# Trainium2, attention and FFN in one kernel: the written-out start is closed to later work, weights are converted in wider chunks, and the start's order is planned anew

## The chip, the cores and the metric

The kernel runs on one core of one Trainium2 chip. The metric is the device time of one execution in microseconds (us), the median of three. A core has five engines that run in parallel, each strictly in its own order: TensorE (PE in the profile) for matmuls, VectorE (DVE), ScalarE (ACT), GpSimd (POOL) and SyncE (SP), which here only issues DMA transfers. An instruction that needs another engine's result waits, and everything behind it on its engine waits with it.

## What is computed

```
x  = out_up + out_local                  # attention, 8 batches x 8 heads, 576 positions, 64 wide
     out_local: softmax over |i - j| < 4 (banded), times v
     out_up:    attention on means of 4 positions, each row repeated 4 times
x  -> (4608, 512)                        # rows = batch x position, columns = head x 64
h  = x @ w_in                            # (4608, 2048)
g  = s * relu(h)**2 + b
out = g @ w_out                          # (4608, 512)
```

`w_in` and `w_out` arrive as 64-bit floats, everything else in 32 bits.

## The kernel before

**FFN.** The 4608 rows are cut into 18 token tiles `t` of 256 and the 2048 FFN columns into 8 "f pairs" `p` of 256. One step `(t, p)` has four parts, which the written-out order calls by one letter. `G` is half of the first product: 12 matmuls into the accumulator `ph` (L622), so 24 for a step; values are split into a high and a low part and three products are summed. `R` is `upper`: Relu, Square and the high part `gh` on ScalarE (L635 to L637). `V` is `lower`: the low part `gl` on VectorE (L642), called the eviction below. `H` is half of the second product into `po` (L684 to L686), 6 matmuls. The term `b` is added at the end as `b` times the column sums of `w_out`: `add_rows(p)` adds up the rows of one pair's `wo` on VectorE (L656, L658, tile `bias`), four adds for a pair, and `column_sums` makes `cs` of them with one matmul (L662), ahead of the second product of step (0, 7).

**Weights.** The 64-bit values of pairs 0 to 6 land in staging tiles `wst` (1024 values a partition for `w_in` and as many for `w_out`) and are converted by `convert` in chunks of 512 columns, so two chunks of each. A chunk runs through ScalarE and VectorE in turn over a scratch tile `es`: scale (L246, ScalarE), two tensor-scalar operations (L248, L249, VectorE), two scalar-tensor-tensor operations (L251, L252, VectorE), a cast to the high part (L254, ScalarE), and the low part by subtraction (L258, VectorE). `es` is one of two buffers of the tag `pv`. Pair 7 is loaded in eight quarters of 256 columns into the same two `pv` buffers and converted by `split_w(7)`.

**Attention.** A unit is a pair of heads of one batch; its parts are `d` (the attention on means), `v` (the sums of `v`, on GpSimd) and `l` (the banded part). The result is `x`; `begin_x` splits the first two token tiles into `xh` and `xl` (L742, L744), `third_x` the third (L752, L754), into buffers of the tags `os` and `xl2`.

**What sets the order.** The order of the first 14 steps, of eight attention units and of pairs 0 to 6 is written out in the string `PLAN`: each word advances one stream (`c` and a number is a weight chunk, `d`, `l`, `v` and a number a unit, `x` and `y` are `begin_x` and `third_x`, then `G`, `R`, `V`, `H`). The instructions traced for it are chained by `in_order`, which makes each follow the one before it on its engine. What is traced afterwards (steps 14 onwards, `split_w(7)`, `add_rows`, the later units) is not chained: a list scheduler places it by priority, and may put it between instructions of the written-out order where it reckons that the engine would wait. The tail of that code:

```
    begin = 2 * HF
    for st in range(begin, len(order)):
        t, p = order[st]
        until("G", 2 * st + 2)
        ...
        if st == begin:
            split_w(NFP - 1)
        if st - begin < NFP:
            add_rows(st - begin)
```

The steps run in this order: tiles 0 and 1 over pairs 0 to 6 (the 14 of the written-out order), then tile 2 over pairs 0 to 6, then tiles 0 to 2 on pair 7, then one tile after the other.

Of the kernel before, what the change touches and what calls it, by code (L numbers as in the profile page):

```python
# [11 lines left out]
F32 = mybir.dt.float32  # L12
# [4 lines left out]
ALU = mybir.AluOpType  # L17
AX = mybir.AxisListType

P = 128  # L20
B, H, S, D = 8, 8, 576, 64
# [17 lines left out]
NFP = DFF // 256  # L39
# [8 lines left out]
NQ = SD // GQ  # L48

STAGE = (7, 6, 7, 6, 7, 6, 7)  # L50
CHUNK = 512
HF = 7
GROUPS = [(i // HP, i % HP // 2) for i in range(EU, B * HP, 2)]

W_MAX = (1.875 - 2.0 ** -23) * 2.0 ** (31 - 127)

PLAN = (
# [16 lines left out]
)  # L74

OB = {0: (0, 1), 1: (2, 3), 2: (6, 7)}
# [3 lines left out]
def attention_ffn_kernel(ctx, tc, qk, vw_in, vr_in, vdm, qkn, vn, w_in, w_out, s_in, b_in, out):  # L80
    nc = tc.nc
# [3 lines left out]
    one = ctx.enter_context(tc.tile_pool(name="one", bufs=1))  # L85
    two = ctx.enter_context(tc.tile_pool(name="two", bufs=2))
# [141 lines left out]
    def load_quarter(p, op, i):  # L228
        if op == "i":
            src = src_i[:, i, 512 * p : 512 * p + 512]  # L230
        else:
            src = src_o[:, 2 * p + i // 2, 512 * (i % 2) : 512 * (i % 2) + 512]
        st = two.tile([P, 256, 2], I32, tag="pv", name="wst")
        nc.sync.dma_start(st.rearrange("p f t -> p (f t)"), src)
        return st

    def convert(st, hi, lo, op, p):


        n = hi.shape[1]  # L240
        top, low = st[:, :, 1], st[:, :, 0]
        f = two.tile([P, n], F32, tag="pv", name="es")
        w = f.bitcast(I32)


        nc.scalar.mul(f, top.bitcast(F32), 2.0 ** -112)  # L246
        yield
        nc.vector.tensor_scalar(f, f, W_MAX, -W_MAX, ALU.min, ALU.max)  # L248
        nc.vector.tensor_scalar(w, w, 3, 0x7FFFFFF8, ALU.logical_shift_left, ALU.bitwise_and)  # L249
        yield  # L250
        nc.vector.scalar_tensor_tensor(w, low, 29, w, ALU.logical_shift_right, ALU.bitwise_or)  # L251
        nc.vector.scalar_tensor_tensor(w, top, -0x80000000, w, ALU.bitwise_and, ALU.bitwise_or)  # L252
        yield
        nc.scalar.copy(hi, f)  # L254
        yield
        for i in range(0, n, 512):
            js = slice(i, min(i + 512, n))
            nc.vector.tensor_tensor(lo[:, js], f[:, js], hi.bitcast(F32)[:, js], ALU.subtract)  # L258

    def split_w(p):  # L260
        for chunk in split_parts(p):
            for _ in chunk:
                pass

    def split_parts(p):
        wi[p] = one.tile([P, 2, NK, 256], F32R, tag=f"wi{p}", name="wi")
        wo[p] = one.tile([P, 2, 2, DM], F32R, tag=f"wo{p}", name="wo")
        for op, w in (("i", wi[p]), ("o", wo[p])):
            fl = w.rearrange("p s k f -> p s (k f)")
            if p < len(STAGE):  # L270
                st = wst.pop((p, op))
                for j in range(0, 1024, CHUNK):
                    js = slice(j, j + CHUNK)
                    yield convert(st[:, js], fl[:, 0, js], fl[:, 1, js], op, p)
            else:
                for i in range(4):
                    cs = slice(256 * i, 256 * i + 256)
                    yield convert(load_quarter(p, op, i), fl[:, 0, cs], fl[:, 1, cs], op, p)
# [311 lines left out]
    def split_x(t):  # L590
        tags = ("os", "xl2") if t == 2 else ("xh", "xl")
        pool = one if t == 2 else two
        xh = pool.tile([P, HP, TB], F32R, tag=tags[0], name="xh")
        xl = pool.tile([P, HP, TB], F32R, tag=tags[1], name="xl")
        t0 = t * TB
        while t0 < (t + 1) * TB:
            b = t0 // S
            while (b, HP - 1) not in complete:
                next(gen)
            n = min((t + 1) * TB, (b + 1) * S) - t0  # L600
            src = xt[b][:, :, t0 - b * S : t0 - b * S + n]
            dst = slice(t0 - t * TB, t0 - t * TB + n)
            nc.scalar.copy(xh[:, :, dst], src)
            nc.vector.tensor_tensor(
                xl[:, :, dst], src, xh[:, :, dst].bitcast(F32), ALU.subtract)
            t0 += n
        xs[t] = (xh, xl)
# [43 lines left out]
    def add_rows(p):  # L651


        parts = [wo[p][:, i // 2, i % 2].bitcast(F32) for i in range(4)]
        if p == 0:
            nc.vector.tensor_tensor(bias, parts.pop(), parts.pop(), ALU.add)  # L656
        for part in parts:
            nc.vector.tensor_tensor(bias, bias, part, ALU.add)  # L658
# [55 lines left out]
    tail = {}  # L714
    ENGINES = [e.engine for e in (nc.tensor, nc.vector, nc.scalar, nc.gpsimd)]
# [67 lines left out]
    def all_chunks():  # L783
        for p in range(HF):
            if p > 1:
                load_w(p)
            if 1 < p < 4:
                load_pair(1, p)
            yield from split_parts(p)
# [13 lines left out]
    with tc.high_priority(offset=400):  # L803
        with in_order():
            for name in plan:
                next(streams[name], None)

    gone = {kind: plan.count(kind) for kind in "GRVH"}

    def until(kind, count):  # L810
        while gone[kind] < count:
            next(streams[kind])
            gone[kind] += 1
# [19 lines left out]
    def target(st):  # L833
        return sum(
            min(1.0, max(0.0, (st - free[b]) / (need[b] - free[b]))) * NY[b]
            for b in range(1, B))

    def advance(st):
        nonlocal done
        while done < target(st):  # L840
            with tc.high_priority(offset=300 if done < NY[1] else 60 if done < NY[1] + NY[2] else 0):
                if next(gen, "end") == "end":
                    break
            done += 1

    splits = {(2, NFP - 2): 3}
    splits.update({(t, NFP - 3): t + 1 for t in range(3, NB - 1)})
    begin = 2 * HF
    for st in range(begin, len(order)):
        t, p = order[st]  # L850
        until("G", 2 * st + 2)
        with tc.high_priority():
            until("R", st + 1)
            until("V", st + 1)
        if st == begin:
            split_w(NFP - 1)
        if st - begin < NFP:
            add_rows(st - begin)
        advance(st + 0.5)
        until("H", 2 * (st + 1 - (2 if t < 3 else 3)))  # L860
        advance(st + 1)
        if (t, p) in splits:
            split_x(splits[t, p])
    until("H", 2 * len(order))


# [60 lines left out]
```

## Time and profile before

| what | us |
|---|---|
| median of 3 runs (979.45 to 981.75) | 980.76 |
| the profiled execution | 980.82 |
| its span, first to last instruction | 979.0 |
| TensorE busy | 937.8 (96%) |
| VectorE busy | 647.3 (66%) |
| ScalarE busy | 481.4 (49%) |
| GpSimd busy | 405.9 (41%) |

Busy shares are means over stages with different limits, so the views by stage matter more than this table. PEclk is the share of TensorE's clock that was granted. In a row of groups stand the line, the engine, the operation, output and inputs, the shape and the count; behind the first bar the busy time in us and the mean of one in ns; behind the second the idle time of the engine just before them and what ended it. In a row of stages each engine has its busy time and, in brackets, its number of instructions.

### The profile page before, as it was taken

The numbers are of one execution on the slowest core, as the hardware profiler recorded it, in microseconds if no ns is written. First come the engines' busy times: TensorE is split into PE (matmuls) and PEld (weight loads), VectorE is DVE, ScalarE is ACT, GpSimd is POOL, SyncE is SP. The second block draws the span as 40 slices with busy tenths as digits, with TensorE's granted clock in tenths as the row PEclk, the third lists the DMA queues.
The fourth block names the chain that finished last, engine by engine and source line by source line (L and its number), as shares of the span: only waits on it lengthen the run. The fifth ranks groups of instructions, "written<-read, shape, count | busy, mean of one in ns | idle before, by whom it ended". The sixth has DMA issues, their size and how long they took to land.

```text
span 979.0 us, 18567 instructions
## 1 busy us (share of the span) xinstructions
PE 937.8 (96%) x7316; PEld 842.0 (86%) x7316; DVE 647.3 (66%) x1204; ACT 481.4 (49%) x1161; POOL 405.9 (41%) x440
## 2 busy tenths in 40 slices
PE   5789789999999999999999999999999999999998
PEld 4678677788999999999898899999999999999997
DVE  8999999563558787778787978787978621211111
ACT  7856777453655263645353545454545433333231
POOL 5400112100047668686767786867676300000000
PEclk9689899999999999999999999999999999999999
DMA  9735323221324141423232233332322000000000
GB/s 325 248 114 170 111 66 110 81 73 30 123 85 148 54 135 65 136 65 123 78 113 88 82 118 95 107 114 87 117 71 76 1 22 1 23 1 22 1 23 22
DMA packets 32104, 86.27 MB, mean 88 GB/s; under 512 B 3344, under 2 KB 7952, under 8 KB 32016
## 3 DMA queue, kind: packets, MB, share of 16 engines
q1 hardware_dynamic: 32016, 85.08, 26.5%
q8 instruction: 57, 0.93, 0.4%
q14 instruction: 31, 0.25, 0.1%
HBM read 75.63 MB, written 9.44 MB: 87 GB/s over the span
## 4 chain that ended last, share of the span: by engine, by line
PE 70%; DVE 16%; POOL 4%; DMA 3%; ACT 3%; issue 2%; DVEq 0%; POOLq 0%; SPq 0%; ACTq 0%
PE ph L622 32%; PE po L684 11%; PE po L685 11%; PE po L686 10%; DVE es L251 2%; POOL pr L527 2%; DVE bias L658 2%; DMA tqk<-in_qk_dram 2%; PE sa L334 2%; POOL acc L549 1%; DVE es L252 1%; DVE gl L642 1%; PE up L375 1%; DVE pv L548 1%; PE ot L559 1%
## 5 line engine op out<-in xcount | busy, mean ns | idle before, releaser
L622 PE MATMUL ph<-xh,wi 128*128 128x256 f32 x2176 | 411.7, 283 | 5.0 <-DVE gl L642 2.0
L622 PEld LDWEIGHTS ph<-xh,wi 128*128 128x128 f32 x2176 | 343.8, 190 | 12.5 <-DVE gl L642 2.8
L622 PE MATMUL ph<-xl,wi 128*128 128x256 f32 x1152 | 324.6, 282 | 1.3 <-DVE xl L744 1.3
L527 POOL TENSOR_TENSOR pr<-lqk 128x576 f32<-128x576 f32 x140 | 200.8, 1459 | 72.8 <-DMA lqk<-in_qkn_dram 30.4
L622 PEld LDWEIGHTS ph<-xl,wi 128*128 128x128 f32 x1152 | 218.0, 189 | 6.1 <-DVE xl L744 1.6
L635 ACT ACTIVATE ph<-ph 128x512 f32<-128x512 f32 x144 | 83.7, 582 | 222.9 <-PE ph L622 209.9
L684 PE MATMUL po<-wo,gh 128*128 128x512 f32 x456 | 183.1, 402 | 3.7 <-ACT gh L637 3.6
L685 PE MATMUL po<-wo,gh 128*128 128x512 f32 x456 | 181.4, 398 | 0.0
L686 PE MATMUL po<-wo,gl 128*128 128x512 f32 x456 | 179.1, 398 | 0.6 <-DVE gl L642 0.6
L642 DVE TENSOR_TENSOR gl<-ph,gh 128x512 fp32r<-128x512 f32 x114 | 78.0, 684 | 122.8 <-ACT gh L637 122.6
L549 POOL TENSOR_TENSOR acc<-acc,pv 128x576 f32<-128x576 f32 x80 | 114.5, 1432 | 55.0 <-DVE acc L549 29.1
L529 DVE TENSOR_REDUCE st<-pr 128x9 f32<-128x576 f32 x140 | 105.9, 757 | 38.7 <-POOL pr L527 36.2
L684 PEld LDWEIGHTS po<-wo,gh 128*128 128x128 f32 x456 | 86.5, 190 | 20.3 <-ACT gh L637 4.8
L686 PEld LDWEIGHTS po<-wo,gl 128*128 128x128 f32 x456 | 86.4, 190 | 19.6 <-DVE gl L642 1.6
L685 PEld LDWEIGHTS po<-wo,gh 128*128 128x128 f32 x456 | 86.6, 190 | 14.9
L548 DVE TENSOR_TENSOR pv<-lv,st 128x576 f32<-128x576 f32 x120 | 87.6, 748 | 15.8 <-POOL acc L549 15.3
L637 ACT CAST gh<-ph 128x512 fp32r<-128x512 f32 x114 | 66.9, 587 | 62.4 <-PE po L685 60.8
L636 ACT ACTIVATE ph<-ph 128x512 f32<-128x512 f32 x144 | 83.8, 582 | 3.3
L305 POOL TENSOR_TENSOR dq<-vq 64x64 f32<-64x64 f32 x58 | 21.2, 365 | 121.3 <-PE up L373 118.8
L304 POOL TENSOR_TENSOR dq<-vt 80x64 f32<-80x64 f32 x58 | 19.0, 339 | 105.6 <-PE up L375 103.8
L685 PE MATMUL po<-wo,gb 128*128 128x512 f32 x120 | 46.9, 390 | 0.0
L686 PE MATMUL po<-wo,gb 128*128 128x512 f32 x120 | 46.8, 390 | 0.0
(153 smaller groups left out, 1213.2 us busy)
## 6 DMA issues: line engine op xcount, KB each, us to landing
tqk<-in_qk_dram SPq DMA_DIRECT2D x30, 584.0 KB, 4.0
lqk<-in_qkn_dram SPq DMA_DIRECT2D x20, 768.0 KB, 4.2
lv<-in_vn_dram SPq DMA_DIRECT2D x20, 480.0 KB, 3.4
out_dram<-os SPq DMA_DIRECT2D x17, 512.0 KB, 3.1
wst<-in_moe_w_in_dram SPq DMA_DIRECT2D x7, 1024.0 KB, 5.4
wst<-in_moe_w_out_dram SPq DMA_DIRECT2D x7, 1024.0 KB, 5.0
tvd<-in_vdm_dram SPq DMA_DIRECT2D x29, 160.0 KB, 2.8
tvr<-in_vr_dram SPq DMA_DIRECT2D x29, 128.0 KB, 3.0
```

The costliest lines, as they stand in the source:

```text
L527: nc.gpsimd.tensor_tensor(pr, lqk[:, 0:CH], lqk[:, CH + o : 2 * CH + o], ALU.mult)
L529: nc.vector.tensor_reduce(ls[:, :, o], pr, AX.X, ALU.add)
L548: nc.vector.tensor_tensor(pv, lv[:, o : o + CH], w, ALU.mult)
L549: (nc.vector if o % 3 == 1 else nc.gpsimd).tensor_tensor(acc[:, :, h], acc[:, :, h], pv, ALU.add)
L622: nc.tensor.matmul(ph[:, j], wi[p][:, s, k, f], xk[:, k], start=k == 0 and s == 0 and xk is xh, stop=k == NK - 1 and s == 1)
L635: nc.scalar.activation(ph, ph, AF.Relu)
L636: nc.scalar.activation(ph, ph, AF.Square)
L637: nc.scalar.copy(gh, ph)
L642: nc.vector.tensor_tensor(gl, acc.pop((t, p)), gh.bitcast(F32), ALU.subtract)
L684: nc.tensor.matmul(po[m], gh[:, j, ms], wo[p][:, 0, j], start=first, stop=False)
L685: nc.tensor.matmul(po[m], gh[:, j, ms], wo[p][:, 1, j], start=False, stop=False)
L686: nc.tensor.matmul(po[m], gl[:, j, ms], wo[p][:, 0, j], start=False, stop=last)
```

## The change

Three things. First, the tracing of the ten steps behind the written-out order (steps 14 to 23, with `split_w(7)`, all `add_rows` and the attention units advanced there) is wrapped in `behind_plan`. It gives each of their instructions on the four computing engines a dependency on the last written-out instruction of its engine. The dependency is one of order alone; no semaphore is added. Second, from pair 2 on a weight chunk is 1024 columns wide. Its `es` doesn't fit into `pv` and takes the buffer of the tag `xl2` (for `w_in`) or `os` (for `w_out`), one buffer each; the subtraction is one instruction in place of one for each 512 columns. Third, `PLAN` is new: the chunks are `c0` to `c17` in place of `c0` to `c27`, and the words stand in another order.

```diff
-CHUNK = 512
+WIDE = 2
...
-    "d0 l0 d0 d1 d0 l0 d1 d2 l1 d0 l0 d2 d3 d0 v0 d1 l0 d0 d3 d0 l0 d2 d1 d0 l1 d1 d2 l1 l0 "
...
+    "d0 l0 d1 l1 d1 d2 l2 d1 l1 d2 d3 d0 d2 d1 d3 l0 l1 d1 v2 d2 d0 d2 l1 l2 d1 l1 v1 l3 d1 "
...
-        f = two.tile([P, n], F32, tag="pv", name="es")
+        if n <= 512:
+            f = two.tile([P, n], F32, tag="pv", name="es")
+        else:
+            f = one.tile([P, n], F32, tag="xl2" if op == "i" else "os", name="es")
...
-        for i in range(0, n, 512):
-            js = slice(i, min(i + 512, n))
-            nc.vector.tensor_tensor(lo[:, js], f[:, js], hi.bitcast(F32)[:, js], ALU.subtract)
+        nc.vector.tensor_tensor(lo, f, hi.bitcast(F32), ALU.subtract)
...
-                for j in range(0, 1024, CHUNK):
-                    js = slice(j, j + CHUNK)
+                n = 512 if p < WIDE else 1024
+                for j in range(0, 1024, n):
+                    js = slice(j, j + n)
...
+    @contextlib.contextmanager
+    def behind_plan():
+
+        traced = nc.cur_bb.bb.instructions
+        last = traced[-1]
+        yield
+        start = next(k for k in reversed(range(len(traced))) if traced[k] is last) + 1
+        for i in traced[start:]:
+            if i.engine in ENGINES:
+                tc.add_manual_dep(
+                    i, tail[i.engine].name,
+                    mybir.DependencyInfo(
+                        mybir.DependencyClass.NoSync, mybir.DependencyReason.DATA),
+                    reason="behind_plan")
...
+        with behind_plan() if st < begin + 10 else contextlib.nullcontext():
+            until("G", 2 * st + 2)
...
```

How this moves instructions. The rows give the line, the operation, the output tile and its inputs (with buffer numbers) and the output's shape. Lines of `convert` stand one higher in the changed kernel (L247 to L255), and its subtraction is L257.

VectorE at the second eviction, before:

```order
L258 TENSOR_TENSOR wo_204<-es_865,wo_204 128x512
L658 TENSOR_TENSOR bias_142<-bias_142,wo_204 128x512
L258 TENSOR_TENSOR wo_204<-es_917,wo_204 128x512
L248 TENSOR_SCALAR es_952<-es_952 128x512
L658 TENSOR_TENSOR bias_142<-bias_142,wo_204 128x512
L249 TENSOR_SCALAR es_952<-es_952 128x512
L658 TENSOR_TENSOR bias_142<-bias_142,wo_204 128x512
L251 SCALAR_TENSOR_TENSOR es_952<-wst_205,es_952 128x512
L252 SCALAR_TENSOR_TENSOR es_952<-wst_205,es_952 128x512
L642 TENSOR_TENSOR gl_964<-ph_885,gh_963 128x512
```

The same place, from the first eviction to the second, in the changed kernel:

```order
L642 TENSOR_TENSOR gl_909<-ph_862,gh_908 128x512
L249 TENSOR_SCALAR es_928<-es_928 128x512
L250 TENSOR_SCALAR es_928<-es_928 128x512
L252 SCALAR_TENSOR_TENSOR es_856<-wst_159,es_856 128x512
L253 SCALAR_TENSOR_TENSOR es_856<-wst_159,es_856 128x512
L252 SCALAR_TENSOR_TENSOR es_928<-wst_159,es_928 128x512
L253 SCALAR_TENSOR_TENSOR es_928<-wst_159,es_928 128x512
L642 TENSOR_TENSOR gl_947<-ph_895,gh_946 128x512
```

The row sums (`bias`) between the conversions are gone from here; the chunks of pair 1 are still 512 columns wide.

VectorE between the sixth and the seventh eviction of the changed kernel, conversions of pairs 3 and 4 beside parts of an attention unit:

```order
L249 TENSOR_SCALAR es_1233<-es_1233 128x1024
L250 TENSOR_SCALAR es_1233<-es_1233 128x1024
L252 SCALAR_TENSOR_TENSOR es_1233<-wst_233,es_1233 128x1024
L253 SCALAR_TENSOR_TENSOR es_1233<-wst_233,es_1233 128x1024
L455 STREAM_TRANSPOSE pt_1300<-pl_814 128x384
L437 TENSOR_REDUCE sm_954<-sl0_955 128x6
L438 TENSOR_TENSOR pl_953<-sl0_955,sm_954 128x192
L257 TENSOR_TENSOR wo_232<-es_1200,wo_232 128x1024
L642 TENSOR_TENSOR gl_1282<-ph_1238,gh_1281 128x512
```

Where two instructions of 512 columns stood, one of 1024 stands; the `es` numbers show that one chunk's subtraction (`es_1200`) comes after the next chunk's four operations (`es_1233`).

VectorE at the end of the written-out order, before (the two evictions are the last of the order and the first behind it):

```order
L658 TENSOR_TENSOR bias_142<-bias_142,wo_250 128x512
L642 TENSOR_TENSOR gl_2124<-ph_2015,gh_2123 128x512
L346 RECIPROCAL dsm_2369<-dsm_2369 96x3
L249 TENSOR_SCALAR es_2177<-es_2177 128x256
L437 TENSOR_REDUCE sm_2394<-sl0_2395 128x6
L251 SCALAR_TENSOR_TENSOR es_2177<-wst_2175,es_2177 128x256
L438 TENSOR_TENSOR pl_2393<-sl0_2395,sm_2394 128x192
L252 SCALAR_TENSOR_TENSOR es_2177<-wst_2175,es_2177 128x256
L258 TENSOR_TENSOR wi_2173<-es_2177,wi_2173 128x256
L248 TENSOR_SCALAR es_2187<-es_2187 128x256
L249 TENSOR_SCALAR es_2187<-es_2187 128x256
L642 TENSOR_TENSOR gl_2162<-ph_2129,gh_2161 128x512
```

And in the changed kernel, from the last eviction of the order on:

```order
L642 TENSOR_TENSOR gl_2023<-ph_1983,gh_2022 128x512
L754 TENSOR_TENSOR xl2_1999<-x_252,os_1998 128x4x192
L656 TENSOR_TENSOR bias_142<-wo_202 128x512
L315 TENSOR_REDUCE qd_2273<-tqk_2248 128x144
L317 TENSOR_REDUCE kd_2274<-tqk_2248 128x144
L658 TENSOR_TENSOR bias_142<-bias_142,wo_202 128x512 x2
L658 TENSOR_TENSOR bias_142<-bias_142,wo_204 128x512 x2
L642 TENSOR_TENSOR gl_2082<-ph_2050,gh_2081 128x512
L658 TENSOR_TENSOR bias_142<-bias_142,wo_204 128x512
L249 TENSOR_SCALAR es_2097<-es_2097 128x256
```

Before, 27 of the 31 instructions on `bias` stand ahead of the fifteenth eviction, the last of them, here, on pair 6's `wo_250`. Now the first one follows the last written-out instruction, and five stand ahead of the fifteenth eviction; the quarters of pair 7 (128x256) start behind it. TensorE's order is the same in both from the first product of the 25th step on, beside the column sums `cs`.

More of the change, by code (lines that the diff above doesn't have):

```diff
@@ L850, in attention_ffn_kernel @@
         t, p = order[st]
[L851 to L863, printed above, removed]
+        with behind_plan() if st < begin + 10 else contextlib.nullcontext():
+            until("G", 2 * st + 2)
+            with tc.high_priority():
+                until("R", st + 1)
+                until("V", st + 1)
+            if st == begin:
+                split_w(NFP - 1)
+            if st - begin < NFP:
+                add_rows(st - begin)
+            advance(st + 0.5)
+            until("H", 2 * (st + 1 - (2 if t < 3 else 3)))
+            advance(st + 1)
+            if (t, p) in splits:
+                split_x(splits[t, p])
     until("H", 2 * len(order))
```

28 rows, old and new, of the table PLAN are left out of this document.

## The prediction

> **What bounds the kernel now.** I read the page's slices first, then the busy time by stage, then the groups by shape inside the first stage, then the waits.
>
> ```profile
> PE   5789789999999999999999999999999999999998
> DVE  8999999563558787778787978787978621211111
> ```
>
> A slice is 24.5 us. TensorE (PE) is below nine tenths only in the first slices; from slice 9 on it is full to the end. VectorE (DVE) is the mirror image: full in the first seven slices, then not. So the time after some 236 us is TensorE's, and what can be won lies before.
>
> ```profile
> core 0: us, PE busy (x) PEld busy (x) DVE busy (x) ACT busy (x) POOL busy (x), PEclk, DMA share, GB/s
> 0.00:47.00 47.00, 31.75 (x610) 26.43 (x610) 40.22 (x89) 38.82 (x107) 26.16 (x60) 0.78 0.86 289
> 47.00:175.50 128.50, 111.32 (x1105) 95.22 (x1109) 119.84 (x240) 86.36 (x202) 12.93 (x24) 0.93 0.35 114
> 175.50:236.00 60.50, 56.90 (x556) 48.78 (x555) 30.95 (x74) 27.82 (x66) 4.96 (x12) 0.97 0.23 70
> 236.00:979.00 743.00, 737.78 (x5060) 671.55 (x5058) 456.24 (x805) 328.44 (x787) 361.83 (x344) 1.00 0.22 72
> ...
> 46.92 0.38 PE L622 MATMUL ph<-xh,wi 128*128 128x256 f32 x1
> ...
> 175.46 0.68 DVE L642 TENSOR_TENSOR gl<-ph,gh 128x512 fp32r<-128x512 f32 x1
> ...
> 236.09 0.86 PE cs L662 x2
> ```
>
> The stages are cut at three events: the first FFN matmul (46.92), the fifteenth `gl` eviction, which is the first one behind the written-out order (175.46), and the column sums `cs` (236.09). In 47 to 175.5 VectorE is busy 119.84 of 128.5 us, 93%. TensorE shows 111.32 us busy, but at a granted clock of 0.93, so its work at full speed is 111.32 x 0.93 = 103.5 us, 81% of the stage. ScalarE's 86.36 is far from a bound. After 236 TensorE is busy 737.78 of 743 at clock 1.00; its order there is the same in both programs but for one step's first product, which moves from just behind `cs` to just ahead of it, so I carry these 743 us over unchanged.
>
> ```profile
> PE ph L622 <- DVE gl L642: 2.0, 1, 2.0
> ...
> PE tr L362 <- DVE pl L438: 1.9, 1, 1.9
> ```
>
> These are the longest of TensorE's waits in 25 to 75 and in 75 to 125 us: both on a VectorE result that stood in a queue. That agrees with VectorE as the bound of this stage.
>
> **The change, part by part.** The prices of VectorE's and ScalarE's instructions:
>
> ```profile
> 0.00:175.50 175.50, 17.72 (x26) 0.89 0.49 161
> ...
> L658 DVE TENSOR_TENSOR bias<-bias,wo 128x512 f32<-128x512 f32 x30 | 20.5, 682 | 0.6 <-ACT wo L254 0.5
> L249 DVE TENSOR_SCALAR es<-es 128x512 int32<-128x512 int32 x28 | 12.2, 436 | 0.8
> L249 DVE TENSOR_SCALAR es<-es 128x256 int32<-128x256 int32 x8 | 2.3, 285 | 0.2
> L248 DVE TENSOR_SCALAR es<-es 128x512 f32<-128x512 f32 x28 | 12.1, 432 | 0.0
> L248 DVE TENSOR_SCALAR es<-es 128x256 f32<-128x256 f32 x8 | 2.3, 293 | 8.4 <-ACT es L246 8.4
> L251 DVE SCALAR_TENSOR_TENSOR es<-wst,es 128x512 int32<-128x512 int32 x28 | 19.7, 704 | 0.5
> L251 DVE SCALAR_TENSOR_TENSOR es<-wst,es 128x256 int32<-128x256 int32 x8 | 3.4, 421 | 0.2
> L252 DVE SCALAR_TENSOR_TENSOR es<-wst,es 128x512 int32<-128x512 int32 x28 | 19.9, 711 | 0.9
> L252 DVE SCALAR_TENSOR_TENSOR es<-wst,es 128x256 int32<-128x256 int32 x8 | 3.4, 426 | 0.1
> L258 DVE TENSOR_TENSOR wi<-es,wi 128x512 fp32r<-128x512 f32 x14 | 9.4, 673 | 0.0
> L744 DVE TENSOR_TENSOR xl<-x,xh 128x768 fp32r<-128x768 f32 x2 | 1.9, 951 | 0.0
> L744 DVE TENSOR_TENSOR xl<-x,xh 128x256 fp32r<-128x256 f32 x2 | 0.8, 418 | 0.0
> L246 ACT ACTIVATE es<-wst 128x512 f32<-128x512 f32 x28 | 18.9, 676 | 16.3 <-DVE wo L258 9.4 <-DVE wi L258 4.8 <-issue 2.0
> L246 ACT ACTIVATE es<-wst 128x256 f32<-128x256 f32 x8 | 3.5, 440 | 9.1 <-DMA wst<-in_moe_w_out_dram 5.0 <-DMA wst<-in_moe_w_in_dram 3.0 <-DVE gl L642 0.7
> L254 ACT CAST wi<-es 128x512 fp32r<-128x512 f32 x14 | 8.7, 619 | 9.6 <-DVE es L252 9.6
> L254 ACT CAST wi<-es 128x256 fp32r<-128x256 f32 x4 | 1.6, 407 | 2.1 <-DVE es L252 2.1
> ```
>
> (1) *Bias sums moved behind.* The first row is VectorE's L658 alone: 26 of the 30 row sums ran before the fifteenth `gl`. In the new order four do. 22 x 0.682 = 15.0 us leave VectorE's busiest stage and go to the next. There they are cheap only while TensorE covers them.
>
> (2) *Wide chunks.* Twenty 512-column chunks of f pairs 2 to 6 become ten of 1024. What one instruction less saves is twice the 256 time minus the 512 time: L248 0.154, L249 0.134, L251 0.138, L252 0.141 us. L744's two widths give the subtraction a slope of 0.2665 us per 256 columns and so a fixed part of 0.152. Together 0.72 per pair of chunks, 7.2 us over ten. No row shows 1024 columns of this code: the bounds are 7.2 saved and nothing saved. A loss has a bound too: an eviction that comes up behind a long instruction waits longer, by at most 1.28 - 0.71 = 0.57 us for each of 14 evictions, 8.0 us. I take 7.2, since four of the five operations have two widths measured here. The Trainium skill ("VectorE: DVE Perf Modes", on the fixed extra latency of SBUF-source operations) has two figures for this fixed part, a table's 58 cycles and a fitted 151 at 0.96 GHz; as estimates from that page they would make 50 removed instructions worth 3.0 or 7.9 us, and the rows above stand by the second.
>
> (3) *Quarter chunks of pair 7.* They no longer start inside the stage; before, about one and a half had: 2 x (0.293 + 0.285) + 0.421 + 0.426 + some 0.45 = 2.5 us.
>
> So VectorE's work in the stage falls from 119.84 to 119.84 - 15.0 - 7.2 - 2.5 = 95.1 us, below TensorE's 103.5. **VectorE stops being the bound; TensorE becomes it**, and not all of the 24.7 us can come out. How dense TensorE gets must be taken from stretches of this trace:
>
> ```profile
> 75.00:100.00 25.00, 22.37 (x235) 19.30 (x233) 24.42 (x48) 14.94 (x35) 0.00 (x0) 1.00 0.45 152
> 100.00:125.00 25.00, 20.56 (x165) 17.38 (x166) 24.04 (x48) 17.88 (x44) 3.62 (x6) 0.85 0.36 120
> ...
> 150.00:175.00 25.00, 23.55 (x268) 20.02 (x268) 19.85 (x45) 19.57 (x53) 5.86 (x12) 1.00 0.33 102
> ```
>
> Both of clock 1.00: with VectorE at 98% TensorE reaches 0.895, with VectorE at 79% it reaches 0.942. With 95.1 us in some 111, VectorE will stand near 86%, a little nearer the second. I take 0.93: 103.5 / 0.93 = 111.3 us in place of 128.5, **17.2 less**.
>
> (4) *The stage behind.* From 175.5 to 236 VectorE gets 30.95 + 15.0 + 2.5 = 48.5 us of work, TensorE keeps 56.90 x 0.97 = 55.2. At the same 0.93 it takes 59.4 us, 1.1 less than 60.5. If the bias sums are late instead, `cs` waits for them: with VectorE no denser than 79% (the last row) the stage takes 61.4, 0.9 more.
>
> (5) *Edits at nothing.* The new dependencies carry no wait, they only fix places. The start is planned anew too; VectorE is idle 47 - 40.22 = 6.8 us there, so at most that is won, and I take nothing, with 4 us either way for the range. SyncE issues the first quarter load of pair 7 ahead of four chunk loads of pairs 4 to 6. Its buffer is free once pair 1 is converted, which the order puts ahead of what frees theirs. If that cover went, ScalarE would wait for a chunk's load as it does now for pair 7's, 5.0 + 3.0 us in L246's row of 256 columns.
>
> The sum: -17.2 - 1.1 = -18.3. The profiled execution took 980.82 us (span 979.0), practically the median of 980.76, so 980.8 - 18.3 = **962.5 us**.
>
> **Rivals.**
>
> *B, nearly no waits left.* The waits on VectorE above vanish with the queue. TensorE at 0.97 gives 106.7 and 56.9 us: 21.8 + 3.6 less, 955.4. Against it: no stretch before 200 us shows more than 0.942.
>
> *C, the clock stays as low.* In 100 to 125 the clock was 0.85 where TensorE was busy 82%, and 1.00 where it was busy 89%. If short pauses of the new order keep 0.93, the work is 111.32, not 103.5: 111.32 / 0.93 = 119.7, 8.8 less and nothing more behind, 972.0. The Trainium skill ("TensorE: Matmul & The Clock Gate", part 1) says that the clock falls to half after an idle window of about 3.4 us and returns after a busy one; by that the denser order keeps full speed, which speaks for A and B. The trace agrees so far that clock and busy share go together.
>
> *D, no change.* VectorE's queue was full only because it had filler; the handoffs between engines set the pace, and the gaps reopen where the bias sums stood. TensorE stays at 0.81 of full speed: 980.8. Against it stand the VectorE waits above.
>
> ```profile
> 233.20 2.89 PE ph L622 x24
> ```
>
> *E, slower: the wide chunk delays the weights.* A chunk runs through ScalarE, VectorE and back: 0.676 + 0.432 + 0.436 + 0.704 + 0.711 + 0.619 + 0.673 = 4.25 us at 512 columns, and by the slopes 1.15 + 0.71 + 0.74 + 1.27 + 1.28 + 1.04 + 1.22 = 7.4 at 1024. The first matmuls of a pair could start on half the weights before, now they need all. Where TensorE stands waiting for the chunk, that costs 3.15 us each; VectorE's subtraction then waits for ScalarE's cast with the next `gl` queued behind it. From seven of the ten chunks on (22 us against 18.3) the kernel is slower; with all ten it is 980.8 - 18.3 + 31.5 = 994.0. Against it: in the new order 8 us of VectorE work stand between the last subtraction of pair 2's `wi` and the `gl` that needs it, while TensorE's and ScalarE's part in between is a step's 24 matmuls, 2.89 us (the row above), and three ScalarE passes over 512 columns of some 0.62 (L254), 4.8 us together.
>
> **How the numbers follow.** Forecast A (956 to 971) 0.55; B 0.14; C 0.14; D 0.05; E 0.12. Within 0.2%, 2.0 us, a measurement of this kernel can hardly tell a change from none. Faster: A, B and C, 0.83; same: D, 0.05; slower: E, 0.12. The range takes in B with the start's gain and TensorE's floors (103.5 and 55.2, together 30.3 less, 950.5), and C with a start 4 us longer or some of a load exposed: 949 to 978.5. D and E stay outside.
>
> **What would show it.** Right: no `bias` row before the written order ends; the fifteenth `gl` near 158 us and `cs` near 221, the moved first product of 2.9 us counted, with some 740 us behind it; VectorE near 86% and TensorE at 0.93 in between at a clock near 1.00; 1024-column instructions of 1.27 us on L252 and L253. Wrong: TensorE waiting on `wi` or `wo` at each pair (E), a granted clock under 0.95 (C), `cs` waiting for `bias`, or clearly more than 740 us behind `cs`.

## The result and the profile after

| | before | changed |
|---|---|---|
| median, us | 981.25 (4 runs) | 966.52 (965.86 to 967.25, 4 runs) |
| the profiled execution | 980.82 | 966.4 |
| its span | 979.0 | 964.6 |

The changed kernel is faster: 0.9847 times the time before, 95% interval 0.9822 to 0.9873; in a second session 0.9837 (0.9824 to 0.9851). That is 14.7 us less, where 18.3 were forecast; 966.5 lies in the stated range of 949 to 978.5.

The page of the changed kernel, the slices that answer to those of before (24.1 us each):

```profile
PE   5699999979999999999999999999999999999998
DVE  7999978864577878787777878787878521111121
```

TensorE is full from the third slice on, but for one, the ninth (193 to 217 us); before, it was full from the seventh on (147 us). The busy times by stage, cut at the same events (first FFN matmul, fifteenth `gl`, column sums):

```profile
0.00:49.20 49.20, 29.94 (x614) 25.14 (x615) 43.33 (x92) 39.79 (x110) 24.80 (x60) 0.83 0.83 285
49.20:155.00 105.80, 101.33 (x1033) 88.32 (x1032) 96.36 (x151) 77.83 (x162) 11.92 (x24) 1.00 0.40 132
155.00:225.50 70.50, 63.41 (x649) 54.24 (x648) 50.50 (x110) 35.06 (x89) 5.75 (x12) 0.98 0.20 64
225.50:964.60 739.10, 732.42 (x5027) 666.25 (x5025) 453.72 (x803) 326.40 (x783) 361.81 (x344) 1.00 0.22 73
...
155.07 0.69 DVE L642 TENSOR_TENSOR gl<-ph,gh 128x512 fp32r<-128x512 f32 x1 [0.25 <-ACT gh L637]
```

The second row is the gain: 105.8 us in place of 128.5, the clock at 1.00 in place of 0.93, TensorE at 101.33 / 105.8 = 0.958. The `gl` row shows more than its time: this eviction waited 0.25 us for ScalarE, so VectorE was there first. The third row is the loss: 70.5 us in place of 60.5. Two things are in it. TensorE has more work, 63.41 x 0.98 = 62.1 us at full speed in place of 55.2: the moved first product of 2.9 us, twelve matmuls of second products that now also stand ahead of `cs` (twelve take some 3 us), and some of attention. And TensorE's idle time has gone from 3.6 to 7.1 us. Where it stood idle behind 155 us, and what held ScalarE up there, by the waits:

```profile
PE up L373 <- ACT ptr L368: 3.7, 1, 3.7
PE po L684 <- ACT gh L637: 2.4, 2, 1.2
PE ph L622 <- DVE gl L642: 1.2, 2, 1.0
...
ACT es L247 <- DMA wst<-in_moe_w_out_dram: 7.8, 4, 2.8
ACT es L247 <- DMA wst<-in_moe_w_in_dram: 4.0, 3, 2.0
```

ScalarE waits 11.8 us for the quarter loads of pair 7, where it waited 8.0 before. The chain of work through the last quarters (start, duration, what):

```profile
195.90 2.96 DMA wst<-in_moe_w_out_dram
198.94 0.45 ACT es L247
199.41 0.30 DVE es L249
...
200.21 0.44 DVE es L252
200.67 0.43 DVE es L253
201.12 0.04 issue
201.16 3.10 DMA wst<-in_moe_w_out_dram
...
204.35 0.44 ACT es L247
```

Each load starts only when the conversion before it has read its quarter, 5.3 us from one to the next: a quarter's staging tile and its scratch tile `es` take one `pv` buffer each, and there are two. Behind the last quarter this chain goes on through an attention unit's transpose, four copies and `ptr` to the matmul `up` at 211.41, where TensorE had waited 3.7 us.

Sums and idle times hide where time comes from and goes. The start of the n-th eviction (`gl`) in the timelines shows it, since all kernels run the same 144 steps:

| profiled run | 15th | 24th | 36th | 71st | 144th |
|---|---|---|---|---|---|
| before | 175.5 | 244.5 | 323.8 | 538.9 | 967.6 |
| changed | 155.1 | 228.9 | 308.1 | 524.4 | 953.2 |
| changed, again (e10) | 155.3 | 229.2 | 308.4 | 523.2 | 951.9 |
| gain of the change | 20.4 | 15.6 | 15.7 | 14.5 | 14.4 |

20.4 us are won by the fifteenth eviction, 4.8 are given back by the 24th, and a further one later. This count is free of what moved across `cs`.

### The profile page after: what moved, and what is told of

The parts are those of the page before. It is cut to its first block, busy times and chain, and to the rows that moved or that the text cites. A ratio compares the mean times of both kernels' runs of the same rounds, so it can differ in the third digit from the quotient of the medians.

```text
span 964.6 us, 18495 instructions
## 1 busy us (share of the span) xinstructions
PE 927.1 (96%) x7316; PEld 834.0 (86%) x7316; DVE 643.9 (67%) x1154; ACT 479.1 (50%) x1141; POOL 404.3 (42%) x440
## 4 chain that ended last, share of the span: by engine, by line
PE 72%; DVE 14%; POOL 4%; DMA 4%; issue 3%; ACT 2%; DVEq 0%; POOLq 0%; SPq 0%; ACTq 0%
PE ph L622 33%; PE po L684 11%; PE po L685 11%; PE po L686 11%; POOL pr L527 2%; POOL acc L549 2%; PE sa L334 2%; DMA tqk<-in_qk_dram 2%; DVE es L252 1%; DMA wst<-in_moe_w_out_dram 1%; DMA lqk<-in_qkn_dram 1%; DVE es L253 1%; PE sl L431 1%; PE up L375 1%; DVE st L529 1%
## 5 line engine op out<-in xcount | busy, mean ns | idle before, releaser
L548 DVE TENSOR_TENSOR pv<-lv,st 128x576 f32<-128x576 f32 x120 | 87.6, 748 | 19.2 <-POOL acc L549 18.8
L685 PE MATMUL po<-wo,gb 128*128 128x512 f32 x120 | 46.9, 391 | 0.0
```

Source lines behind the costliest of these rows:

```text
L548: nc.vector.tensor_tensor(pv, lv[:, o : o + CH], w, ALU.mult)
L685: nc.tensor.matmul(po[m], gh[:, j, ms], wo[p][:, 1, j], start=False, stop=False)
```

## The experiments

The theory (Q) was that VectorE's queue bounds the written-out stretch and that bias sums kept out of it are the gain; the rivals, that the new order is (O), or that TensorE sets the stretch by now and VectorE's share is spare (P). For what was given back: the serial load chain of the quarters (L), or the bias sums moved there (S). Each run is quoted with what was written ahead of it. Eviction starts are those of its profiled run, as in the table above.

**e1, the closing alone.** The kernel before, with `behind_plan`, this line and nothing else:

```diff
+        with behind_plan() if st < begin + 10 else contextlib.nullcontext():
```

> The kernel before with nothing but the closing: its old order and 512-column chunks, the later work kept behind. Theory Q (VectorE's queue bounds the written-out stretch): 15.0 us of bias sums and 2.5 us of quarters leave the stretch, VectorE has about 102 us of work there, the fifteenth gl comes 11 to 15 us earlier than at 175.5, some 4 us are given back behind it; in all 7 to 12 us less than the kernel before (about 969 to 974). Rival O (it is the new order that wins, the closing is idle): within 3 us of the kernel before.

971.38 us, ratio 0.990 (0.9881 to 0.9918). Fifteenth eviction 159.0, 24th 229.9. The closing alone brings 16.5 of the 20.4 us by the fifteenth eviction, more than expected; 1.9 of them are given back by the 24th and 5.1 by the 144th (956.2). The closing keeps bias sums, quarters and parts of later attention units out of the stretch together; no run keeps out the bias sums alone. Stage rows, to the fifteenth eviction and from there:

```profile
46.70:159.00 112.30, 104.77 (x1046) 90.69 (x1037) 105.37 (x205) 81.10 (x185) 12.33 (x24) 0.98 0.39 131
159.00:230.00 71.00, 64.72 (x658) 55.38 (x658) 48.93 (x110) 36.08 (x92) 5.61 (x12) 1.00 0.20 63
```

**e2, all but the closing.** The changed kernel with

```diff
-        with behind_plan() if st < begin + 10 else contextlib.nullcontext():
+        with contextlib.nullcontext():
```

> The changed kernel without the closing: the scheduler may again put bias sums and quarters between the written-out instructions. Theory Q: VectorE's work before the fifteenth gl rises by about 15 us, from 96 to about 111 in a stretch of 106, so the stretch is 8 to 13 us longer, and since the stage behind is lighter again in all 5 to 10 us more than the changed kernel (about 972 to 977). Rival O: within 3 us of the changed kernel's 966.5.

977.66 us, 0.9968 (0.9955 to 0.9981), a little slower than expected. Fifteenth eviction 173.9, 18.8 later than in the changed kernel, of which 2.8 arise ahead of the first FFN matmul (52.0 in place of 49.2); VectorE's busy time to there is back at 116.66 us:

```profile
52.00:173.90 121.90, 107.34 (x1133) 92.11 (x1132) 116.66 (x201) 82.82 (x182) 15.76 (x24) 0.97 0.38 125
```

O falls by both runs: without the closing, new order and wide chunks are worth 0.3%.

**e3, the wide instructions halved.** Each operation of `convert` runs over two halves of a chunk, one behind the other, before the next operation does:

```diff
-        nc.scalar.mul(f, top.bitcast(F32), 2.0 ** -112)
+        for js in parts:                      # halves of 512 columns
+            nc.scalar.mul(f[:, js], top[:, js].bitcast(F32), 2.0 ** -112)
...
```

> The changed kernel with every 1024-column instruction of the conversion issued as two of 512, all else and the order as they are. Theory Q: 50 instructions more on VectorE at 0.14 to 0.15 us, 7.2 us more in a stretch where VectorE has 96.4 of 105.8 us: 103.6 leaves almost no slack, so the stretch is 3 to 6 us longer, 969 to 973 in all. Rival E (a long instruction holds up evictions): the shorter instructions win, 966 or less. Rival P (TensorE alone sets the stretch now): no more than 2 us longer.

968.64 us, 0.9885 (0.9866 to 0.9905). Its fifteenth eviction is at 155.7, its 24th at 228.1, beside 155.1 and 228.9 of the changed kernel: in the part that the wide chunks are for, the wide instructions bring 0.6 us and then nothing. The rest of what the time is longer by comes later (144th: 955.4). Its first stage:

```profile
49.30:155.70 106.40, 101.09 (x1033) 88.20 (x1032) 97.94 (x201) 79.76 (x182) 11.05 (x24) 1.00 0.40 131
```

VectorE has 50 instructions more than the changed kernel (201 against 151) and is busy 97.94 us in place of 96.36: 0.03 us for each, not 0.14. TensorE is busy 101.09 of 106.4, and the stretch is 0.6 us longer (the whole kernel 2.1), as theory P says. But the run put 1.6 us more on VectorE and not the expected 7.2, so it tests P with no more than that. Why so little, the starts on VectorE show, of one pair of chunks before, one wide chunk in the changed kernel, and its halves in e3 (x2 marks two in a row):

```profile
86.86 0.42 DVE L248 TENSOR_SCALAR es<-es 128x512 f32<-128x512 f32 x1
87.31 0.43 DVE L249 TENSOR_SCALAR es<-es 128x512 int32<-128x512 int32 x1
87.77 0.69 DVE L251 SCALAR_TENSOR_TENSOR es<-wst,es 128x512 int32<-128x512 int32 x1
88.50 0.69 DVE L252 SCALAR_TENSOR_TENSOR es<-wst,es 128x512 int32<-128x512 int32 x1
89.11 0.42 DVE L248 TENSOR_SCALAR es<-es 128x512 f32<-128x512 f32 x1
...
91.36 0.68 DVE L642 TENSOR_TENSOR gl<-ph,gh 128x512 fp32r<-128x512 f32 x1
```

```profile
81.13 0.68 DVE L249 TENSOR_SCALAR es<-es 128x1024 f32<-128x1024 f32 x1
81.85 0.69 DVE L250 TENSOR_SCALAR es<-es 128x1024 int32<-128x1024 int32 x1
82.58 1.22 DVE L252 SCALAR_TENSOR_TENSOR es<-wst,es 128x1024 int32<-128x1024 int32 x1
83.83 1.22 DVE L253 SCALAR_TENSOR_TENSOR es<-wst,es 128x1024 int32<-128x1024 int32 x1
84.98 0.55 DVE L448 TENSOR_TENSOR pl<-pl,sm 128x384 f32<-128x384 f32 x1
```

```profile
81.20 0.76 DVE L252 TENSOR_SCALAR es<-es 128x512 f32<-128x512 f32 x2
81.87 0.76 DVE L254 TENSOR_SCALAR es<-es 128x512 int32<-128x512 int32 x2
82.54 1.29 DVE L258 SCALAR_TENSOR_TENSOR es<-wst,es 128x512 int32<-128x512 int32 x2
83.74 1.29 DVE L261 SCALAR_TENSOR_TENSOR es<-wst,es 128x512 int32<-128x512 int32 x2
84.95 0.55 DVE L459 TENSOR_TENSOR pl<-pl,sm 128x384 f32<-128x384 f32 x1
```

An instruction that reads what the one ahead of it wrote starts 0.03 us behind that one's end (88.50 behind 87.77 + 0.69). One that doesn't starts some 0.08 before it (89.11 and 88.50 + 0.69). In e3 each operation runs over both halves before the next begins, so no instruction of such a chunk reads what the one just ahead of it wrote. From the first to what follows, the four operations take 4.50 us for the two chunks before, 3.85 for the wide one and 3.75 in e3. So e3 undoes the width but not what the wide chunks saved on VectorE, and what that is worth in time no run shows.

By the fifteenth eviction the 20.4 us split, taken in this order, into the closing 16.5 (e1), the new order with chunks of 1024 in halves 3.3 (159.0 to 155.7), and the wide instructions 0.6.

**e4, one load for all quarters.** The other seven loads are left out.

```diff
-                    yield convert(load_quarter(p, op, i), fl[:, 0, cs], fl[:, 1, cs], op, p)
+                    if op == "i" and i == 0:
+                        held = load_quarter(p, op, i)
+                    yield convert(held, fl[:, 0, cs], fl[:, 1, cs], op, p)
```

> The changed kernel, but pair 7's first quarter is loaded once and converted eight times, so seven of its eight loads are left out (the values of pair 7 are not the reference's). Theory L (behind the fifteenth gl, the serial chain load, convert, load of the quarters holds up VectorE and ScalarE, and with them TensorE): the stage from the fifteenth gl to the column sums shortens by 4 to 6 us from 70.5, 960.5 to 962.5 in all. Rival S (the bias sums moved there fill VectorE): no change beyond 1.5 us, 965 to 968.

962.67 us, 0.9812 (0.9794 to 0.9829). Fifteenth eviction 155.3, 24th 221.4, so 7.5 earlier than in the changed kernel:

```profile
155.30:221.40 66.10, 64.16 (x658) 55.10 (x657) 50.12 (x110) 36.41 (x91) 6.01 (x12) 1.00 0.13 40
```

TensorE is at 0.97 here, and VectorE has nearly as much work as in the changed kernel up to its 24th eviction (50.12 us, there 52.61). L holds: the stage to `cs`, for which 4 to 6 us were expected, is 4.7 shorter (`cs` at 221.2). At the end 3.3 us are left (144th: 949.9).

**e5 and e11, the control.** To give the quarters a scratch tile of their own, 1 KB of a partition had to come free. The control frees it by summing `v` in place:

```diff
-        vt = tmp([P, 2, P], "vt")
-        vq = tmp([P, 2, D], "vq")
+        if b == 0 and hp:
+            vt, vq = tmp([P, 2, P], "vt"), tmp([P, 2, D], "vq")
+        else:
+            vt, vq = tvd[:, 0:2], tvr[:, 0:2]
```

> A control for the next run: the changed kernel, but the sums of v are written over the loaded tiles instead of into tiles of their own, which frees 1.5 KB of a partition. No theory expects an effect: 965 to 968.5.

> The control with the sums of v in place once more; it was 960 where no effect was expected. If the scheduler's other order of the later units is the reason, it is so again: 958.5 to 962, 5 to 7 us below the changed kernel beside it. If it was the chip or the day, it is within 2 us of it.

959.93 us, 0.9788 (0.9763 to 0.9813); again 959.66, 0.9771 (0.9758 to 0.9785), beside the changed kernel's 966.32 on the same chip. That was a miss: the control is the fastest kernel of the study. Little of it is the part under study: beside the changed kernel's first trace the fifteenth eviction is 0.8 and 1.2 us earlier, the 24th 3.7 and 1.8, the 71st 9.9 and 7.3. TensorE's order behind the closed part is another in the control's traces. Which exchange of instructions brings the gain is open, and so is whether the order brings it or the in-place sums themselves; no run took it apart.

**e6, an own scratch tile for the quarters**, on top of the control:

```diff
-            f = two.tile([P, n], F32, tag="pv", name="es")
+            f = (two if n == 512 else one).tile([P, n], F32, tag="pv" if n == 512 else "eq", name="es")
```

> As the control, and the quarters of pair 7 convert in a scratch tile of their own, so both pv buffers hold loads and the next load no longer waits for the conversion of the quarter before. Nothing is left out. Theory L (the serial load chain costs the stage behind the fifteenth gl 4 to 6 us): 961 to 964, near the run with one load, and ScalarE's wait of 11.8 us on the loads falls under 4. Rival S: no more than 1.5 us below the control.

965.16 us, 0.9843 (0.982 to 0.9866). In the stage it does what L says: 24th eviction at 219.8, 9.0 earlier than in the changed kernel and 5.3 and 7.3 earlier than in the two runs of the control, no wait of ScalarE on a quarter load, TensorE busy 63.93 of 65.3:

```profile
154.50:219.80 65.30, 63.93 (x658) 54.93 (x657) 49.38 (x110) 36.54 (x91) 5.87 (x12) 1.00 0.20 65
...
PE ph L624 <- DVE gl L644: 4.8, 6, 2.7
```

The second line is TensorE's longest wait between 400 and 800 us in this run: evictions late in a later stage, where the scheduler's order is another again. At the end 3.2 us are left beside the changed kernel, and the whole is 5.2 us slower than its control (959.93). So L is shown for the stage, but not as a gain in the total.

**e7, the row sums on GpSimd** (`nc.gpsimd` in `add_rows`) in the changed kernel, and **e8**, the same on top of e6:

> The changed kernel with the 31 row sums on GpSimd, which is busy 5.75 of 70.5 us in the stage behind. Theory L: the row sums were not what held TensorE there; within 2 us of the changed kernel, 964.5 to 968.5, and ScalarE still waits some 12 us on the quarter loads. Rival S (the moved bias sums fill VectorE): 4 to 5 us less, 961 to 963.

> Own scratch tile for the quarters and the row sums on GpSimd together. Theory L: as the run with the own scratch tile, 960 to 964. If both theories hold a part, it is the fastest, 958 to 961.

e7: 975.39 us, 0.9946 (0.9925 to 0.9968); 24th eviction 239.4, 10.5 later. e8: 965.62 us, 0.9848 (0.9822 to 0.9873). Both missed, and e7 says nothing on S, for it slows VectorE down. Groups of 155 to 215 us, of e7 and then of the changed kernel:

```profile
L658 POOL TENSOR_TENSOR bias<-bias,wo 128x512 f32<-128x512 f32 x22 | 28.8, 1308 | 18.0 <-ACT wo L255 16.6
L250 DVE TENSOR_SCALAR es<-es 128x256 int32<-128x256 int32 x8 | 6.9, 860 | 0.1
L252 DVE SCALAR_TENSOR_TENSOR es<-wst,es 128x256 int32<-128x256 int32 x8 | 6.5, 809 | 0.2
L642 DVE TENSOR_TENSOR gl<-ph,gh 128x512 fp32r<-128x512 f32 x6 | 4.1, 684 | 3.7 <-ACT gh L637 3.6
```

```profile
L252 DVE SCALAR_TENSOR_TENSOR es<-wst,es 128x256 int32<-128x256 int32 x8 | 3.5, 436 | 0.1
L250 DVE TENSOR_SCALAR es<-es 128x256 int32<-128x256 int32 x8 | 2.3, 289 | 0.1
```

The conversion of the quarters takes two and three times as long while GpSimd adds; the eviction, which reads `ph` from PSUM, the accumulators' memory, keeps its 684 ns. e8 has the same, with 598 and 833 ns for L250 and L252.

**e9, no row sums** but the first; the kernel leaves the rest of that term out:

```diff
-        parts = [wo[p][:, i // 2, i % 2].bitcast(F32) for i in range(4)]
+        parts = [wo[p][:, i // 2, i % 2].bitcast(F32) for i in range(4)][: 2 if p == 0 else 0]
```

> The changed kernel without 30 of the 31 row sums (the term b is then wrong, all else is computed). Theory L: they fill VectorE behind the written-out stretch but hold up nothing there; the ninth eviction after the fifteenth (gl 24 of 144) comes no more than 2 us earlier than at 228.9, and the kernel takes 964 to 968. Rival S: 18.8 us of VectorE work less give 4 to 6 us there, 960.5 to 962.5.

963.11 us, 0.9802 (0.9783 to 0.9822). Fifteenth eviction 155.3, 24th 226.9, 2.0 earlier, 144th 949.9, 3.3 earlier. Between the two expectations: the moved sums cost something where they stand now, some 2 us in the stage, of which the scheduler's other order there may be a part. In this stage the load chain is the larger of the two: 7.5 us by e4, 5.3 to 9.0 by e6.

**e10, the changed kernel again; e12, an own scratch tile for the four `w_out` quarters alone:**

> The changed kernel once more, on the same chip as the runs beside it: 965 to 968, ratio 0.984 to 0.987 to the kernel before.

> As the control, with an own scratch tile for the four w_out quarters alone. Theory L: the loads' wait on the w_out quarters (7.8 of 11.8 us) goes, 3 to 5 us less at gl 24 than the control; what the later stage makes of it depends on the order that the scheduler finds there: 956 to 964.

e10: 966.32 us, as before. e12: 970.25 us, 0.988 (0.9867 to 0.9894): 24th eviction at 220.9, 4.3 and 6.2 earlier than the two controls (3 to 5 were expected), but 144th at 957.3, 12.9 and 11.2 later than theirs. The total is a miss: more is given back later than the stage won. That the later order does it is not shown.

## Why the prediction was right, and where it was off

**The bound moved as said.** The steps "22 x 0.682 = 15.0 us leave VectorE's busiest stage" and "VectorE stops being the bound; TensorE becomes it" fit the runs: the closing alone brings 16.5 us by the fifteenth eviction (e1), taking it away costs 18.8 there (e2), and TensorE is at 0.958 of the stage. The 15.0 were somewhat high, for the instruction behind a bias sum starts 0.60 us after it in most places, so 22 of them took some 13 us of the queue. VectorE's busy time came out at 96.36 us, forecast 95.1; part of that is luck, since parts of later attention units, some 3 us that the sum did not count, left the stage as well. A range taken from VectorE's 24.7 us alone would have gone too far; TensorE's work at full speed was the right floor. It was 101.3 us, forecast 103.5, because 72 matmuls fewer stand there, most of them of attention units that now come behind.

**The density was a little low.** 0.93 was chosen between two rows of before, by VectorE's share; 0.958 came, with VectorE at 91% and not near 86%. Its share was the wrong guide:

```profile
75.00:100.00 25.00, 25.00 (x214) 22.46 (x213) 24.51 (x32) 19.57 (x37) 0.00 (x0) 1.00 0.48 165
100.00:125.00 25.00, 23.02 (x293) 19.22 (x295) 24.17 (x42) 19.81 (x45) 7.25 (x12) 1.00 0.40 131
```

In the first row VectorE is as full as in the same stretch before (98%), where TensorE reached 0.895, and TensorE is full. The likely reason is that no filler stands ahead of what TensorE waits for; these rows do not prove it. The first stage took 105.8 us, forecast 111.3. The start gave 2.3 us of that back (first FFN matmul at 49.2, not 46.9), where nothing had been taken. The fifteenth `gl` was forecast near 158 and came at 155.1.

**The stage behind was mis-sized: that is the step that failed.** The sum had -1.1 there, because 48.5 us of VectorE work fit beside TensorE's 55.2. VectorE's work was sized rightly (50.50), TensorE's was not: it was 62.1 us, and the moved first product accounts for 2.9 of the 6.9 more. The prediction's "the same in both programs but for one step's first product" overlooked the twelve matmuls of second products that moved with it. Nor was the sum of work the whole question. The quarter conversions, which before had begun inside the written-out stretch and now stand wholly behind it, are a chain of load and conversion with one load in flight, and ScalarE and VectorE stand in order behind each link. Against the kernel before, 4.8 us were lost there between the 15th and the 24th eviction, 3.4 of them in idle time of TensorE; e4 and e6 cut the chain and win 7.5 and 9.0 us by the 24th. The chain does not follow from the closing alone: in e1, where the quarters stand behind it too, 1.9 us were lost, and ScalarE waits 4.9 us for their loads. The line of before had shown it: ScalarE's idle time in L246's row of 256 columns, 5.0 + 3.0 us behind loads. The prediction quoted it as the price of another edit. The `cs` was forecast near 221 and came at 225.7; no wait of it for `bias`, as feared, is in the lists, and without the load chain it came at 221.2 (e4) and 219.6 (e6).

**That the sum came near is in part luck.** By stages, with the moved product counted in the stage behind, the spans moved by +2.2 (start), -22.7, +10.0 and -3.9 us; the forecast had 0, -17.2, +1.8 and -2.9. An error of 5.5 us one way stands against one of 8.2 the other way.

**The wide chunks' 7.2 us were on VectorE, but what they gave in time is open.** Single durations fell as the slopes said (forecast 1.27 us for L252 and L253, the two rows show 1.219 and 1.226):

```profile
L253 DVE SCALAR_TENSOR_TENSOR es<-wst,es 128x1024 int32<-128x1024 int32 x10 | 12.3, 1226 | 0.3
L252 DVE SCALAR_TENSOR_TENSOR es<-wst,es 128x1024 int32<-128x1024 int32 x10 | 12.2, 1219 | 0.1
```

By the starts above, four operations of a wide chunk take 0.65 us less than those of the two chunks before, where these follow one another: 6.5 us over ten, and less where a bias sum stood between them. But e3 shows that it is not the count of instructions that costs: with 50 more, in an order in which none reads what the one just ahead of it wrote, VectorE's busy time rose by 1.6 us. With TensorE busy 101.3 of 105.8 us, no more than 4.5 us were left to win in the stretch. The forecast did not suffer, since its sum went by TensorE's density. From start to start the fixed part of a scalar-tensor-tensor operation is 2 x 0.72 - 1.25 = 0.19 us where the next one reads its result, and 2 x 0.61 - 1.14 = 0.08 where it doesn't. The Trainium skill's two figures for the fixed part ("VectorE: DVE Perf Modes", on the fixed extra latency of SBUF-source operations), 58 and 151 cycles, are as estimates at its 0.96 GHz 0.06 and 0.16 us, each a little below one of these.

**The rivals.** B (955.4) was nearer in the first stage, and TensorE did pass 0.942; its second stage was wrong, as the forecast's was. C falls: the clock was 1.00 in the first stage. D falls by e1. E falls by the lists of waits of the first stage, which have none of TensorE on `wi` or `wo`; and with 512-column instructions (e3) the fifteenth eviction comes no earlier. The 743 us behind `cs` were 739.1, near the 740 said, but with the twelve matmuls gone from there some 737 were due, so some two us are lost again there.

## What to carry to other kernels

Filler that a scheduler finds a gap for on paper can fill the very engine that bounds the stage: look which instructions stand in the bound engine's queue without being waited for there, and close the stretch to them. When work moves into a stage that has room by the sum of busy times, look for chains in it (a load that waits for a buffer, on an engine that others queue behind), for a chain costs by its links and not by its busy time. A bound engine's busy share does not tell how dense the waiting engine can get: with VectorE at 98% TensorE stood at 0.895 before and was full after. Where a list scheduler orders the rest, follow a gain by the same event in both traces to the end, and run an edit that should do nothing beside the one that should.

## What the runs showed of the hardware

- A VectorE instruction that reads what the one just ahead of it wrote starts 0.03 to 0.04 us behind that one's end (all 21 places of L252 behind L251 between 47 and 175 us of the kernel before); one that doesn't, and waits for nothing else, starts 0.07 to 0.08 us before that end (there, what follows each of the 14 evictions). So the order of instructions can save what merging them saves: 50 more cost 1.6 us of busy time in e3.
- GpSimd's additions slow some of VectorE's operations: L250 0.289 to 0.860 us, L252 0.436 to 0.809 (e7), the eviction from PSUM not at all (0.684). The Trainium skill ("GPSIMD Engine Reference", key points) says that GpSimd shares its SBUF interfaces with VectorE and contends with instructions of two SBUF inputs or in a two-port mode. The rows agree for L252, which has two inputs in SBUF; L250 has one, and no run shows in which mode it ran.
- An edit of the sums of `v`, expected to do nothing, moved the kernel by 0.7% (e5, e11); the scheduler's order of the later units was another, and whether that is the reason is open. An effect of that size is not an edit's own until a control has been run.
